# Gate phases of a retention + two-MoE kernel: products of neighbouring quads dealt out among each other, output products as filling, a shorter norm

## The chip, the cores and the metric

One core of a Trainium2 chip. The metric is the device time of one execution in microseconds, from the first to the last instruction and what lies around it; the median of three executions is given. The engines are named as in the profile: PE (TensorE), PEld (its weight loads), DVE (VectorE), ACT (ScalarE), POOL (GpSimd), SP (SyncE, which only issues transfers here).

## The reference

```
attn:  4 batches, 8 heads, 576 positions, head size 64:  ((q k^T / 8) * decay) v,  causal, no softmax
x   =  attn as 2304 tokens x 512
MoE 1: h = x @ w_in (512x2048);  g = h * cos(h);  x = g @ w_out (2048x512)
MoE 2: xn = x / sqrt(mean(x^2) + 1e-6) * rms_g
       out = (silu(xn @ w_gate) * (xn @ w_val)) @ w_out     (512x1536, 512x1536, 1536x512)
```

## The kernel before, in words

All products are fp32 made from three matmuls on high and low parts (`minus` makes a low part on DVE, after ACT has made the high one). The program runs attention, then MoE 1 over five token tiles in the order `ORDER_A` = 0, 1, 2, 4, 3 (four of 512 tokens, tile 4 of 256), then MoE 2 over three groups of 768 tokens (0, 1, 2). The weights of MoE 2 are prepared on the chip and stored to DRAM; later groups load them.

MoE 2 multiplies in Strassen's manner with seven products per 2x2 block. A *gate phase* has twelve *quads* (`quad`, even ones for the gate, odd ones for the value), each with seven products numbered 0 to 6 (`product`). A product is 2 x 3 matmuls of 128x128 weights on 384 columns. A quad owns two PSUM banks, alpha and beta: products 0, 2, 4 and 5 go to alpha, one on top of the other, and 1, 3 and 6 to beta. Between them the partial sum in alpha has to be copied out (`sums_of`: ACT's copies s1 after product 0, s2 after 2, s4 after 4), and `result` adds a sum and beta on DVE; for an even quad ACT takes the Silu of it, for an odd one DVE multiplies it with that Silu. So product 2 waits for s1's copy, product 3 for the add of result (0,0), product 4 for s2's copy, and a later quad's product for the add that last read its bank. Two quads later the banks come round again (`banks`). The order of PE is written out by hand: products 2, 3, 4 of quad q, then 0, 1 of quad q+1, then 5, 6 of quad q. The order of instructions on ACT, DVE and PE is that of the code (manual schedule).

In the *output phase* (`whole_out`) of a group seven `out_product`s of 54 matmuls with 256 columns each follow; the first begins inside the gate phase's end. `out_split` casts SV, the gate phase's result, into high and low parts, `block_out` adds up a block of the output into a tile `o` (two buffers) and stores it. `operand_steps(g+1)` makes the next group's seven token operands meanwhile.

In group 0 the weights of quads 2 to 11 are still made (`quad_steps`: ACT cast, DVE split, four POOL steps, two ACT casts, two DVE splits, two stores, and the fetch of another quad's input z; the first two steps of quad q+2 run after quad q's product 6). Ahead of that, in the last tile of MoE 1, the six output items (`out_steps`) and quads 0 and 1 are made in the same way. `ahead` puts their halves and the first group's operand steps into the list `ready`, which `other_steps` pulls in the order A, D, A, D, D (A an ACT step, D one of DVE) once for each of the sixteen steps of the tile. All output items go through the same staging tile `slots[0]`.

`norm(t)` makes the RMS norm of a tile in steps: squares (ACT), their sum (DVE), the mean over partitions (two matmuls with ones), an integer first guess of the inverse root, three Newton iterations of three DVE steps, and four scalings of x. It runs as `background` that `idle` takes up one step at a time: tiles 0, 1 and 2 in MoE 1, tiles 4 and 3 in group 1.

Of the kernel before, what the change touches and what calls it, by code (L numbers as in the profile page):

```python
# [22 lines left out]
F32 = mybir.dt.float32  # L23
# [7 lines left out]
P = 128  # L31
# [49 lines left out]
def body(ctx: ExitStack, tc, qkv, qkr, vr, w1, w2, rg, gq, gk, mask, out):  # L81
# [43 lines left out]
    spare = const.tile([P, 1], F32, name="spare")  # L125
    xall = const.tile([P, KC, NT], F32, name="xall")
# [94 lines left out]
    nc.vector.memset(quarter, 0.25)  # L221
    nc.gpsimd.memset(ones_r.bitcast(F32), 1.0)
# [94 lines left out]
    nc.sync.dma_start(rg_sb, rg)  # L317

# [4 lines left out]
    def norm(t):  # L323
# [21 lines left out]
        def mean():  # L345
            st["mean"] = acc_tile(0) if "S" in late else ps_tile()
            late["held"] = True
# [3 lines left out]

        def guess():
            late["held"] = False
            m, y = tmp(), tmp()
            nc.vector.tensor_scalar(m[:, :n], st["mean"][:, :n], 1.0 / DM, EPS, op0=ALU.mult, op1=ALU.add)
            nc.vector.tensor_scalar(y[:, :n].bitcast(I32), m[:, :n].bitcast(I32), -0.5, 1597463007.0,
                                    op0=ALU.mult, op1=ALU.add)
            st["m"], st["y"], st["u"] = m[:, :n], y[:, :n], tmp()[:, :n]

        def newton(step):  # L360
            m, y, u = st["m"], st["y"], st["u"]
            if step == 0:
                nc.vector.tensor_tensor(u, y, y, op=ALU.mult)
            elif step == 1:
                nc.vector.scalar_tensor_tensor(u, u, -0.5, m, op0=ALU.mult, op1=ALU.mult)
            else:
                nc.vector.scalar_tensor_tensor(y, u, 1.5, y, op0=ALU.add, op1=ALU.mult)
# [25 lines left out]
    def pull(engine):  # L393

        for steps in (background, ready) if late.get("held") else (ready, background):
# [114 lines left out]
    def operand_weights(q, plain, sums, keep_plain, keep):  # L510
# [17 lines left out]
        def low1():  # L528
            z = values_of.pop(q)
            for n in range(2):  # L530
                minus(nc.vector, sums[:, 1, 2 * n:2 * n + 2], sums[:, 0, 2 * n:2 * n + 2], z[:, 3 * n:3 * n + 2])
            keep()

        return [("A", high0), ("D", low0), ("A", high1), ("D", low1)]
# [84 lines left out]
    def ahead(i, n):  # L619
# [20 lines left out]
    def out_t(t, f):  # L640
# [9 lines left out]
        if f == NF1 - 1:  # L650
# [7 lines left out]
            if t not in ORDER_A[-2:]:  # L658
# [362 lines left out]
```

## Time and profile before

| | |
|---|---|
| median of three executions | 928.43 us (926.58 to 929.02) |
| the profiled execution | 930.18 us; its span, first to last instruction, 928.4 us |
| PE busy | 892.3 us, 96% of the span |
| DVE, ACT, POOL busy | 674.4, 474.6, 94.1 us |
| granted PE clock, mean | 0.993 of full speed |
| DMA | 189 MB, 204 GB/s over the span |

The stages of the span: attention and MoE 1 up to 494.1 us, gate phases from 494.1, 647.1 and 786.2, output phases from 606.1, 745.2 and 884.0. A row of a timeline has the start and the length in us, the engine, the line, the instruction with what it writes and reads, the count of merged instructions, and in brackets how long the engine stood before it and what ended that. Matmuls are pipelined and their ends are modelled: pace is read from start to start.

### The profile page before, as it was taken

What the parts mean: (1) busy time and instruction counts of PE and PEld (TensorE: products, weight loads), DVE (VectorE), ACT (ScalarE), POOL (GpSimd) and SP (SyncE); (2) the same over time, 40 slices, a digit from 0 to 9 for tenths busy, and PEclk for the clock granted to TensorE, in tenths of its full rate; (3) what the DMA queues carried; (4) which work ended last, traced back from release to release, by engine and by line L of the source; (5) the groups of instructions that cost most, each with busy time, mean ns of one, the idle gap of its engine ahead of it and who ended that gap; (6) DMA issues with size and microseconds to landing.
All of it is one profiled execution on the core that took longest, in us unless ns stands there. A gap on an engine that the chain in (4) does not pass through costs nothing.

```text
span 928.4 us, 14258 instructions
## 1 busy us (share of the span) xinstructions
PE 892.3 (96%) x5482; PEld 808.3 (87%) x5482; DVE 674.4 (73%) x1013; ACT 474.6 (51%) x813; POOL 94.1 (10%) x99
## 2 busy tenths in 40 slices
PE   7899999999999999999997999899999999999998
PEld 6788888888887888988886899899999999899998
DVE  3999989678788886678887576688467688343484
ACT  4666575566555664466554555444333344333341
POOL 2330100000000000002245333100000000000000
PEclk9999999999999999999999999999999999999999
DMA  8956261145434543104479788888666588666593
GB/s 335 413 213 247 102 250 47 34 140 163 140 101 125 147 141 89 46 7 133 144 229 322 265 295 291 320 289 274 242 238 241 213 290 281 235 238 243 211 291 118
DMA packets 59027, 188.98 MB, mean 204 GB/s; under 512 B 5328, under 2 KB 23376, under 8 KB 50384
## 3 DMA queue, kind: packets, MB, share of 16 engines
q1 hardware_dynamic: 58960, 188.08, 58.9%
q8 instruction: 43, 0.70, 0.3%
q14 instruction: 24, 0.20, 0.1%
HBM read 140.87 MB, written 47.19 MB: 203 GB/s over the span
## 4 chain that ended last, share of the span: by engine, by line
PE 60%; DVE 21%; ACT 7%; DMA 6%; issue 4%; SPq 1%; POOL 1%; ACTq 0%; DVEq 0%
PE acc L836 11%; PE h L771 11%; PE acc L771 11%; PE acc L192 5%; PE acc L193 5%; PE acc L194 5%; DVE w L129 3%; DVE r L429 2%; DVE t L147 2%; PE h L836 2%; DVE glo L129 2%; PE h L193 2%; PE h L194 2%; PE h L192 2%; DVE r L423 2%
## 5 line engine op out<-in xcount | busy, mean ns | idle before, releaser
L771 PE MATMUL h<-w 128*128 128x384 f32 x720 | 139.7, 344 | 9.7 <-DVE SV L780 5.4
L771 PE MATMUL acc<-w 128*128 128x384 f32 x720 | 137.1, 337 | 10.4 <-ACT s L756 10.3
L771 PEld LDWEIGHTS h<-w 128*128 128x128 f32 x720 | 128.8, 193 | 12.7 <-DVE SV L780 6.6
L771 PEld LDWEIGHTS acc<-w 128*128 128x128 f32 x720 | 126.0, 189 | 13.9 <-ACT s L756 13.6
L192 PE MATMUL acc<-ghi,w 128*128 128x512 f32 (+1 forms) x320 | 117.4, 373 | 2.7 <-ACT xall L652 1.7
L193 PE MATMUL acc<-glo,w 128*128 128x512 f32 (+1 forms) x320 | 117.8, 370 | 0.6 <-DVE glo L129 0.5
L194 PE MATMUL acc<-ghi,w 128*128 128x512 f32 (+1 forms) x320 | 117.4, 368 | 0.0
L836 PE MATMUL acc<-w 128*128 128x256 f32 x846 | 105.1, 285 | 0.0
L836 PEld LDWEIGHTS acc<-w 128*128 128x128 f32 x846 | 104.1, 194 | 0.2
L425 ACT ACTIVATE r<-r,half_pi 128x512 f32<-128x512 f32 (+1 forms) x80 | 54.5, 681 | 67.6 <-DVE r L423 67.3
L520 POOL TENSOR_TENSOR z<-z 128x256 f32<-128x256 f32 x72 | 64.5, 903 | 171.4 <-DMA z<-w 81.7
L129 DVE TENSOR_TENSOR glo<-r,ghi 128x512 fp32r<-128x512 f32 (+1 forms) x78 | 52.5, 673 | 35.4 <-ACT ghi L431 35.1
L431 ACT CAST ghi<-r 128x512 fp32r<-128x512 f32 (+1 forms) x80 | 46.2, 578 | 52.8 <-DVE r L429 50.9
L192 PEld LDWEIGHTS acc<-ghi,w 128*128 128x128 f32 x320 | 59.3, 188 | 14.5 <-ACT xall L652 2.6
L785 DVE TENSOR_TENSOR v<-s,acc 128x384 f32<-128x384 f32 x54 | 29.8, 551 | 57.7 <-ACT s L756 45.0
L193 PEld LDWEIGHTS acc<-glo,w 128*128 128x128 f32 x320 | 60.3, 188 | 11.0 <-DVE glo L129 1.2
L194 PEld LDWEIGHTS acc<-ghi,w 128*128 128x128 f32 x320 | 60.3, 188 | 10.1
L819 ACT CAST w<-SV 128x768 fp32r<-128x768 f32 x55 | 42.5, 832 | 41.3 <-DVE SV L787 23.1
L781 ACT ACTIVATE SV<-SV 128x384 f32<-128x384 f32 x54 | 28.4, 526 | 65.8 <-DVE SV L780 65.8
L780 DVE TENSOR_TENSOR SV<-s,h 128x384 f32<-128x384 f32 x54 | 29.7, 550 | 39.1 <-ACT s L756 31.2
L129 DVE TENSOR_TENSOR w<-SV,w 128x768 fp32r<-128x768 f32 x55 | 50.0, 951 | 9.9 <-ACT w L819 9.9
L756 ACT COPY s<-h 128x384 f32<-128x384 f32 x54 | 25.8, 477 | 56.1 <-PE h L771 56.1
(117 smaller groups left out, 1684.2 us busy)
## 6 DMA issues: line engine op xcount, KB each, us to landing
w<-so SPq DMA_DIRECT2D x42, 768.0 KB, 5.6
w<-s SPq DMA_DIRECT2D x24, 1024.0 KB, 4.9
raw<-w_dram SPq DMA_DIRECT2D x36, 512.0 KB, 4.2
w<-s SPq DMA_DIRECT2D x24, 768.0 KB, 6.0
raw<-w_dram SPq DMA_DIRECT2D x16, 1024.0 KB, 6.9
x<-qkv_dram SPq DMA_DIRECT2D x15, 1024.0 KB, 11.2
s<-w SPq DMA_DIRECT2D x12, 1024.0 KB, 6.3
w<-t SPq DMA_DIRECT2D x36, 256.0 KB, 2.4
```

The source lines that it names most:

```text
L129: eng.tensor_tensor(dst, src, hi.bitcast(F32), op=ALU.subtract)
L192: nc.tensor.matmul(dst, a[0], b[0], start=start, stop=False)
L193: nc.tensor.matmul(dst, a[0], b[1], start=False, stop=False)
L194: nc.tensor.matmul(dst, a[1], b[0], start=False, stop=stop)
L425: nc.scalar.activation(r, r, AF.Sin, bias=half_pi, scale=1.0)
L431: nc.scalar.copy(hi, r)
L520: nc.gpsimd.tensor_tensor(z[:, dst], z[:, a], z[:, b], op=op)
L771: nc.tensor.matmul(bank, a[:, wp], xp[:, c], start=start and kc == 0 and m == 0, stop=kc == 1 and m == 2, skip_group_check=True)
L780: nc.vector.tensor_tensor(dst, s, bank, op=ALU.add)
L785: nc.vector.tensor_tensor(t, s, bank, op=ALU.add)
L819: nc.scalar.copy(t[:, 0], src)
L836: nc.tensor.matmul(bank, s[:, a, i % 2, m * P:(m + 1) * P], wi[:, b], start=start and i == 0 and p == 0 and m % 2 == 0, stop=i == NPR - 1 ...
```

## The change

- `quad` becomes a class whose `product(k)` also does what follows the product on ACT and DVE. The loop deals two quads out among each other: 0, 1 of quad q, 5 of quad q-1, 2, 3 of q, 6 of q-1, 4 of q.
- A Silu goes to a list `waiting` and is issued right after the next sums copy (`flush`). s2 gets two buffers.
- In groups 1 and 2, where quad 0 has no quad before it, parts of the last output product of the group before stand in the places of 5 and 6; the last block's adds and store follow there. At the end of a gate phase the first 36 of the first output product's 54 matmuls, which stood in one piece ahead of products 5 and 6 of the last quad, stand in two pieces of 18 around product 5. The `o` tiles come from a pool of three.
- The output items are drawn more evenly, the second split of a quad's weights is cut into two steps, and the steps of `quad_steps` are spread over the seven places of a quad.
- The norm of the third tile of the order moves from the last tile of MoE 1 into group 0's gate phase (tiles 3 and 4 stay in group 1, in that order). Its iteration has seven DVE steps instead of nine; the mean's scaling and epsilon go to ACT; a factor 0.375 goes into `rg_sb` once.

```diff
-        steps += [("A", high), ("D", low), None, None, ("P", mean), None, None, ("D", guess)]
-        if t in ORDER_A[-2:]:
+        steps += [("A", high), ("D", low), None, None, ("P", mean), None, None, ("A", square_mean), ("D", guess)]
+        if t in ORDER_A[2:]:
...
-        steps += [("D", lambda s=s: newton(s)) for _ in range(3) for s in range(3)]
+        steps += [("D", lambda s=s: refine(s)) for s in range(7)]
...
-        for _ in range((n > 0) + (n in (8, 10, 12))):
+        for _ in range((n > 0) + (n % 3 == 0 < n)):
             ready.extend(next(halves, []))
-        if 1 <= n < 8:
+        if n in (1, 2, 4, 5, 7, 8, 10):
...
+    def flush():
+        while waiting:
+            waiting.pop(0)()
+
+    def sums_of(name, bank, width=GROUP):
+        t = sp.tile([P, width], F32, tag=name, name=name)
         nc.scalar.copy(t[:, :HALF], bank)
+        flush()
...
+        def product(self, k):
...
+            if k == 0:
+                self.s[1] = sums_of("s1", self.alpha)
+            elif k == 1:
+                self.result(0, 0, self.s[1], self.beta)
+            elif k == 2:
+                self.s[2] = sums_of(*(("s2", self.alpha) if self.q % 2 else ("s3", self.alpha, HALF)))
+            elif k == 4:
+                self.s[4] = sums_of("s4", self.alpha)
+                self.result(1, 1, self.s[4], self.beta)
+            elif k == 5:
+                self.result(0, 1, None, self.alpha)
+                flush()
+            elif k == 6:
+                self.result(1, 0, self.s[2], self.beta)
+                fetch(self.n + 3)
...
-        out_product(g, 6, delta, True)
-        block_out(g, 1, 0, s2, delta)
-        run(s[16:17])
...
+        out_product(g, 6, delta, True, range(NPR) if last else range(2))
...
+        def second():
+            out_product(g, 6, delta, True, range(4, NPR))
+            block_out(g, 1, 0, s2, delta)
+            late["last"] = s[16:]
+
+        late["fill"] = [lambda: out_product(g, 6, delta, True, range(2, 4)), second]
...
+            if q < NQUAD - 2 and k == 4:
+                items.append(quad_steps(q + 2))
+                run(items[-1][:1])
+            if 0 < q < NQUAD - 1:
+                run({0: items[-1][1:2], 3: items[-1][2:3], 6: items[-1][3:4]}.get(k, []))
+                if k == 4:
+                    run(items[-2 if q < NQUAD - 2 else -1][4:5])
...
+            now = Quad(g, q)
+            for k in (0, 1, 5, 2, 3, 6, 4):
+                if k < 5:
+                    now.product(k)
+                elif before:
+                    before.product(k)
+                elif fill:
+                    fill.pop(0)()
+                hook(g, q, k)
...
+                late["op"] = pool("op", 3)
+        late["alpha"] = [acc_tile(0), acc_tile(1)]
+        out_product(g, 0, late["alpha"], True, range(2))
+        hook(g, NQUAD, "first")
+        before.product(5)
+        out_product(g, 0, late["alpha"], True, range(2, 4))
+        before.product(6)
```

What this does to the order on the engines, at three places.

PE, from the end of group 0's output phase into group 1 (first before, then after). `h` and `acc` are the PSUM banks, 384 columns are gate products, 256 columns output matmuls.

```order
L836 MATMUL acc<-w 128x256 x144
L836 MATMUL acc<-w,b 128x256 x18
L836 MATMUL acc<-w 128x256 x18
L771 MATMUL h<-w 128x384 x30
L771 MATMUL acc<-w 128x384 x12
L771 MATMUL h<-w 128x384 x12
```

```order
L851 MATMUL acc<-w 128x256 x144
L806 MATMUL h<-w 128x384 x12
L851 MATMUL acc<-w,b 128x256 x18
L806 MATMUL h<-w 128x384 x12
L851 MATMUL acc<-w 128x256 x18
L806 MATMUL h<-w 128x384 x6
L806 MATMUL acc<-w 128x384 x12
```

The five products of quad 0 ran in one piece (30 matmuls); now 18 output matmuls stand after products 0, 1 and 18 more after 2, 3.

DVE at the same place: L862 and L877 are the adds of `block_out`, L780 and L788 the add of result (0,0) of quad 0.

```order
L862 TENSOR_TENSOR o<-s_5878,acc 128x256
L129 TENSOR_TENSOR w<-xall,w 128x768
L600 TENSOR_TENSOR xall<-xall 128x2x384
L129 TENSOR_TENSOR w<-xall,w 128x768 x2
L862 TENSOR_TENSOR o<-s_5746,acc 128x512
L862 TENSOR_TENSOR o<-s_5746,acc 128x256
L780 TENSOR_TENSOR SV<-s_5970,h 128x384
```

```order
L877 TENSOR_TENSOR o<-s_5878,acc 128x256
L130 TENSOR_TENSOR w<-xall,w 128x768
L610 TENSOR_TENSOR xall<-xall 128x2x384
L130 TENSOR_TENSOR w<-xall,w 128x768 x2
L788 TENSOR_TENSOR SV<-s_5926,h 128x384
L338 TENSOR_TENSOR nt<-nt 128x512
L877 TENSOR_TENSOR o<-s_5746,acc 128x512
L877 TENSOR_TENSOR o<-s_5746,acc 128x256
```

The add of quad 0 now stands ahead of the last block's adds.

ACT in the middle of group 0, from an even quad's s2 to the odd quad's s4. `s` are the sums copies, `SV<-` the Silus, `w<-z` the casts of `quad_steps`.

```order
L756 COPY s_5073<-h 128x384
L756 COPY s_5087<-h 128x384
L781 ACTIVATE SV<-SV 128x384
L526 CAST w<-z 128x512 x2
L756 COPY s_5106<-acc 128x384
L781 ACTIVATE SV<-h 128x384
L781 ACTIVATE SV<-SV 128x384
L514 CAST w<-z 128x768
L756 COPY s_5145<-acc 128x384
L756 COPY s_5159<-acc 128x384
```

```order
L772 COPY s_5052<-h 128x384
L535 CAST w<-z 128x512 x2
L772 COPY s_5079<-h 128x384
L523 CAST w<-z 128x768
L772 COPY s_5095<-acc 128x384
L790 ACTIVATE SV<-SV 128x384
L790 ACTIVATE SV<-h 128x384
L772 COPY s_5127<-acc 128x384
L535 CAST w<-z 128x512 x2
L772 COPY s_5152<-acc 128x384
L790 ACTIVATE SV<-SV 128x384
L523 CAST w<-z 128x768
```

The Silu that waits for product 6's add stood two places ahead of the odd quad's s2; it now stands behind that quad's s4.

## Rows read from the trace of the kernel before

**Rows 1.** The page: busy us, share of the span, instructions of each engine.

```profile
PE 892.3 (96%) x5482; PEld 808.3 (87%) x5482; DVE 674.4 (73%) x1013; ACT 474.6 (51%) x813; POOL 94.1 (10%) x99
```

**Rows 2.** The chain that ended last: start us, us, what.

```profile
496.19 4.49 DMA z<-w
...
695.03 2.08 PE acc L771 x12
```

**Rows 3.** Stages: us, busy us (instructions) of PE, PEld, DVE, ACT, POOL, granted clock, DMA.

```profile
410.00:494.10 84.10, 83.59 (x374) 68.71 (x372) 69.79 (x98) 52.49 (x85) 26.23 (x26) 1.00 0.52 164
494.10:606.10 112.00, 98.94 (x542) 94.22 (x541) 73.32 (x107) 54.95 (x106) 38.22 (x47) 0.97 0.82 295
606.10:647.10 41.00, 41.00 (x343) 40.92 (x343) 37.91 (x40) 19.87 (x29) 0.00 (x0) 1.00 0.88 290
647.10:745.20 98.10, 94.80 (x547) 93.80 (x546) 56.87 (x104) 36.33 (x75) 0.00 (x0) 0.98 0.65 234
786.20:884.00 97.80, 94.01 (x543) 93.36 (x542) 38.27 (x66) 32.26 (x65) 0.00 (x0) 0.98 0.65 234
```

**Rows 4.** The same view for the quads' matmuls alone (PE, PEld).

```profile
647.10:656.00 8.90, 7.12 (x31) 6.83 (x32) 0.81 0.84 305
656.00:736.00 80.00, 79.62 (x457) 78.74 (x455) 1.00 0.64 233
```

**Rows 5.** Timeline of PE, start of group 0.

```profile
496.19 0.62 PE L771 MATMUL h<-w 128*128 128x384 f32 x2 [1.77 <-ACT w L514]
...
501.06 4.97 PE L771 MATMUL h<-w 128*128 128x384 f32 x18 [1.87 <-ACT s L756]
...
516.45 2.25 PE L771 MATMUL h<-w 128*128 128x384 f32 x12
```

**Rows 6.** Groups of ACT, 480 to 505 us: busy us, mean ns, idle before.

```profile
L526 ACT CAST w<-z 128x512 fp32r<-128x512 f32 x6 | 3.6, 619 | 8.4 <-DMA so<-w 5.0 <-POOL z L520 3.4
```

**Rows 7.** Timeline of ACT, a pair of quads and the end of group 0.

```profile
529.92 0.81 ACT L514 CAST w<-z 128x768 fp32r<-128x768 f32 x1
530.65 0.47 ACT L756 COPY s<-acc 128x384 f32<-128x384 f32 x1
...
593.86 0.83 ACT L819 CAST w<-SV 128x768 fp32r<-128x768 f32 x1 [1.71 <-DVE SV L787]
```

**Rows 8.** Timeline of PE, gaps after that.

```profile
531.17 1.32 PE L771 MATMUL acc<-w 128*128 128x384 f32 x6 [1.02 <-ACT s L756]
...
597.12 1.59 PE L771 MATMUL acc<-w 128*128 128x384 f32 x6 [2.50 <-ACT s L756]
...
652.17 3.88 PE L771 MATMUL h<-w 128*128 128x384 f32 x12 [1.75 <-DVE SV L780]
...
737.60 1.33 PE L771 MATMUL acc<-w 128*128 128x384 f32 x6 [1.54 <-ACT s L756]
...
791.75 3.59 PE L771 MATMUL h<-w 128*128 128x384 f32 x12 [2.26 <-DVE SV L780]
```

**Rows 9.** Timeline of DVE, start of group 1.

```profile
650.64 1.02 DVE L862 TENSOR_TENSOR o<-s,acc 128x512 f32<-128x512 f32 x2 [4.04 <-DMA out_dram<-o]
651.57 0.55 DVE L780 TENSOR_TENSOR SV<-s,h 128x384 f32<-128x384 f32 x1
```

**Rows 10.** A pair of quads in group 0, columns as in rows 3.

```profile
531.00:546.70 15.70, 14.86 (x84) 14.50 (x84) 10.57 (x17) 8.68 (x18) 6.01 (x8) 1.00 0.86 306
```

**Rows 11.** A norm step on DVE, 470 to 512 us: ns, min/median/max.

```profile
L363 DVE TENSOR_TENSOR nt<-nt x2: 680/952/1225, 471.3 to 491.5; 128x512 f32<-128x512 f32 x2
```

**Rows 12.** Timeline of POOL, one quad's four steps.

```profile
531.88 3.27 POOL L520 TENSOR_TENSOR z<-z 128x256 f32<-128x256 f32 x4 [5.40 <-DVE w L129]
```

**Rows 13.** Transfers issued from 470 to 610 us: KB each, us to landing.

```profile
so<-w SPq DMA_DIRECT2D x15, 256.0 KB, 4.7
```

**Rows 14.** Timeline of ACT, the second cast of quad 0's weights.

```profile
499.50 1.14 ACT L526 CAST w<-z 128x512 fp32r<-128x512 f32 x2 [3.36 <-POOL z L520]
```

**Rows 15.** Loads of quad weights in group 1, issue to landing.

```profile
DMA to landing us min/median/max: 4.6/5.3/6.8
```

More of the change, by code (lines that the diff above doesn't have):

```diff
@@ L393, in pull @@
     def pull(engine):
-        for steps in (background, ready) if late.get("held") else (ready, background):
+        for steps in (ready, background):
             if steps and steps[0] and steps[0][0] == engine:
@@ L526, in high1, with low1 @@
                 nc.scalar.copy(sums[:, 0, 2 * n:2 * n + 2], z[:, 3 * n:3 * n + 2])
[L528 to L534, printed above, removed]
+        def low1(n):
+            z = values_of[q]
+            minus(nc.vector, sums[:, 1, 2 * n:2 * n + 2], sums[:, 0, 2 * n:2 * n + 2], z[:, 3 * n:3 * n + 2])
+            if n:
+                del values_of[q]
+                keep()
+        return [("A", high0), ("D", low0), ("A", high1), ("D", lambda: low1(0)), ("D", lambda: low1(1))]
     where = lambda q: 3 * (q // 2) + q % 2
@@ L733, in body @@
         ready.pop(0)[1]()
+    assert not background and next(halves, None) is None
     staging.close()
@@ L752, in run, with __init__, result @@
             step()
-    def sums_of(name, bank):
-        t = sp.tile([P, GROUP], F32, tag=name, name=name)
+    def flush():
[3 more added lines that the diff above has]
+        t = sp.tile([P, width], F32, tag=name, name=name)
         nc.scalar.copy(t[:, :HALF], bank)
+        flush()
         return t[:, :HALF]
-    def quad(g, q, hook):
-        val, j = q % 2, q // 2
-        n = g * ITEMS + q
-        alpha, beta = (t[:, :HALF] for t in banks())
-        plain, sums = side(n)
-        def product(bank, w, k, start):
-            home, xhi, xlo = ops[g, k]
-            for kc in range(2):
-                a, c = w[..., kc * P:(kc + 1) * P], kc
-                for m, (wp, xp) in enumerate(((0, xhi), (0, xlo), (1, xhi))):
-                    nc.tensor.matmul(bank, a[:, wp], xp[:, c], start=start and kc == 0 and m == 0,
-                                     stop=kc == 1 and m == 2, skip_group_check=True)
-            if q == NQUAD - 1:
-                places.append(home)
-        def result(u, h, s, bank):
-            dst = SV[:, j, u, h]
-            if not val:
+    class Quad:
+        def __init__(self, g, q):
+            self.g, self.q, self.n = g, q, g * ITEMS + q
+            self.plain, self.sums = side(self.n)
+            self.alpha, self.beta = (t[:, :HALF] for t in banks())
+            self.s = {}
+        def result(self, u, h, s, bank):
+            dst = SV[:, self.q // 2, u, h]
+            if self.q % 2 == 0:
                 if s is not None:
                     nc.vector.tensor_tensor(dst, s, bank, op=ALU.add)
-                nc.scalar.activation(dst, bank if s is None else dst, AF.Silu)
+                    bank = dst
+                waiting.append(lambda: nc.scalar.activation(dst, bank, AF.Silu))
             else:
@@ L859, in block_out @@
     def block_out(g, dm, half, a, pair):
-        o = gp.tile([P, GROUP], F32, tag="o", name="o")
+        o = late["op"].tile([P, GROUP], F32, tag="o", name="o")
         for c, bank in zip(PARTS, pair):
@@ new lines, in body @@
+    items = []
+    for g in range(NGROUP):
+        assert not background
+        for t in (ORDER_A[2:3], ORDER_A[:2:-1], [])[g]:
+            background.extend(norm(t))
+        fill = late.pop("fill", [])
+        before = None
+        for q in range(NQUAD):
+            now = Quad(g, q)
[7 more added lines that the diff above has]
+                hook(g, q, k)
+            before = now
+            if g == 0 and q == NQUAD - 2:
```

133 lines of the change are left out of this document (57 added, 76 removed).

## The prediction, made before the changed kernel ran

> **What bounds the kernel now.** I read the page's busy shares first, then the stages in one windows view, then for each stage that loses time the timelines of the engines that TensorE (PE) waits for. PE is busy 96% of 928.4 us, DVE 73%, ACT 51% [rows 1], so only stretches where PE is not at its own pace can be won. One product of a quad is 6 matmuls; 12 of them run back to back in 2.08 us [rows 2], so a product takes 1.04, and an output matmul 41.0 / 343 = 0.12 [rows 3]. Each of the three gate phases has 84 products and the first 36 output matmuls: 87.4 + 4.3 = 91.7 us. They take 112.0, 98.1 and 97.8 [rows 3]; the second also holds the matmuls of two norm means (some 0.7). The loss is 20.3 + 5.7 + 6.1 = 32 us. The output phases (41.0 busy of 41.0) and the middle of group 1's gate phase (79.62 of 80.0) lose nothing [rows 3, 4]. The change is judged by what it takes from those 32 us.
>
> **Where the 32 us are.** *Start of group 0* (494.1 to 516.45): 12 products, 12.5 us of work, in 22.35: 9.9 lost. PE waits 1.77 for quad 0's weights and 1.87 for a sums copy, and then 18 matmuls take 4.97 where 12 take 2.25 at pace [rows 5]: after such gaps the granted clock falls from the upper of its two levels (2.4 GHz) to the lower (1.2); the mean over the stretch of the like gap in group 1 is 0.81 [rows 4]. Ahead of those weights stand ACT's waits for stores to land, because all six output items go through one staging tile: 5.0 us [rows 6]. *Rest of group 0*: 72 products and the 36 matmuls, 79.2 us, take 89.65: 10.4 lost. The repeating part: after an even quad ACT runs, in order, the Silu of product 6's result, quad q+2's first weight cast (0.81) and only then the copy of product 2's partial sum, which PE's product 4 awaits: 1.02 us of gap in the pair of quads shown [rows 7, 8], and about as much in every pair. At the end, ACT waits 1.71 for DVE before a cast that stands ahead of the same copy; PE stands 2.50 [rows 7, 8], and the slow matmuls behind the gap cost more. *Groups 1 and 2*: at the start DVE stands 4.04 us for an output store that still reads one of two o tiles, with the add that frees product 1's bank queued behind it. PE waits 1.75 and 2.26, then needs 3.88 and 3.59 for 12 matmuls: 3.4 and 3.6 lost. At the end of group 1 the same queue on ACT costs 1.54 again [rows 8, 9], and I take group 2 for like it.
>
> **The change, part by part.**
>
> *Start of groups 1 and 2.* The o pool has three tiles, so the last block writes the tile whose store went out with the group's first block, some 20 us before, and DVE's wait goes. Two thirds of the last output product move to where a preceding quad's products 5 and 6 would stand; the same 54 matmuls run. What is late next: product 3 needs the add of result (0,0). From the end of the fourth output product DVE has two blocks' o adds, three weight splits and a difference to do, about 6.7 us with the copy before them (the two adds of a block take 1.02 [rows 9]; a split or difference of 768 columns some 0.95, an estimate, a little under twice the 0.55 of a 384-column add there), and PE passes 2.2 + 2.1 + 2.2 + 1.0 = 7.5 before product 3. Then quad 1's product 0 takes over the bank that the last block's adds (1.02) read, with one product between: at best even. I leave 0.5 us for both. Gain 2.9 and 3.1; bounds 1.5 each (a wait of 2 us comes back) and the whole 3.4 and 3.6.
>
> *End of the gate phases.* Product 4 now follows product 2 after two others (3 of its own quad, 6 of the one before), 2.08 us, where 1.04 stood, and the casts of the output's first operand stand behind the copies. I leave 0.2 at each end. Gain 1.3 in groups 1 and 2 each, bounds 0.5 and 1.7. Their middles, without loss today, can only lose: each bank now has 2.08 us from one product's end to the next one's start on it. A copy and an add of 384 columns, 0.47 and 0.55 [rows 7, 9], with some 0.3 to start, fit in; I book nothing.
>
> *Rest of group 0.* The Silu is put off until behind the next copy, so the repeating wait goes. What is late next is DVE. In the pair of quads from 531.0 to 546.7 it is busy 10.57 of 15.7 us [rows 10]; at PE's pace a pair has 14.57. The norm of the third tile moves here: 16 DVE steps, two or three a quad in quads 5 to 9. The same steps took 0.68 alone and 1.22 beside POOL [rows 11]. Five a pair make 10.57 + 3.4 = 14.0 to 10.57 + 6.1 = 16.7: 0 to 2.1 over PE's pace. POOL works 3.27 us of a quad's 7.3 [rows 12], so some half of the steps meet it: 1.1 a pair, 2.7 for two and a half pairs, and about 1 for order in the other quads. With 0.3 for the end, 4.0 of the 10.4 stay: gain 6.4, bounds 1 (every step beside POOL and ahead of an add that frees a bank) and 9.5.
> On that the Trainium skill (SBUF — State Buffer, Who interferes with whom) has a rule that speaks against the move: a DVE instruction with two SBUF inputs and a GpSimd instruction that reads SBUF shut each other out for a whole instruction. The trace agrees in kind, 0.68 against 1.22. By the rule each of the 16 could be held for one POOL step, 3.27 / 4 = 0.82, which makes 13 us of DVE; by the rows' difference it is 16 × 0.54 = 8.6 at most.
>
> *Start of group 0.* The output items are drawn at steps 3, 6, 9 and 12 of the last tile rather than 8, 10 and 12, so item 4's sums cast stands two steps before item 5's, some 10.8 us (48 matmuls at 84.1 / 374 = 0.225 [rows 3]), where one step stood. A store lands 4.7 us after issue [rows 13], and its four issues take some 2: 6.7, inside two steps and outside one. The 5.0 us of waits go. In their place: PE runs products 0 and 1 from about 494. Product 2 needs the copy of product 0, which now stands behind quad 1's first cast. That waits for its input, which is fetched when item 5's weights are done and lands 4.5 us later [rows 2]; it was asked for at 496.2 and is now some 3.8 earlier (most of the 5.0; behind item 5's first cast POOL's work takes the place of the stores), so it lands at 497. With 0.83 and 0.48 for cast and copy product 2 can start at 498.4; before, it began at 501.06 [rows 5]. Product 4's copy now stands behind quad 1's second cast, which waits for POOL as quad 0's does (3.36 [rows 14]), so it ends near 503.5. From there eight products without a wait bring the twelfth to 511.8 instead of 516.45. Gain 4.7, bounds 0 (the waits only move) and 7.
>
> *The norm itself.* Nine steps of Newton become seven, and ACT takes the mean's scaling: DVE loses three steps of 0.68 a tile, ACT gains one. Up to 494.1 PE is busy 83.59 of 84.1 [rows 3], so there is next to nothing to win, and slack on both engines covers the added ACT step: 0 to 0.5. Without that cover it would cost 0.6 for each of two tiles.
>
> **Sum.** 2.9 + 3.1 + 1.3 + 1.3 + 6.4 + 4.7 = 19.7. The profiled execution took 930.18 us, so 910.5; it lay 1.75 above the median of the runs, 928.43, so **908.7 us** for the median.
>
> **Rivals.**
> *A, DVE becomes the bound of group 0.* If most norm steps meet POOL and stand ahead of adds that free banks, quads 5 to 9 run at 8.3 us, and the start of the group gains little (ACT has new squares there). Against it: DVE has 5.1 us spare in a pair today. Gain 2.9 + 3.1 + 2.6 + 1 + 2 = 11.6: 916.8.
> *B, one wait takes the place of another at the starts.* The banks of the last output product are read in quad 0's middle; if its adds come late there, quad 1 stands as quad 0 did. For it: by the count above DVE's queue there is full to within a microsecond. The starts then win 1.5 each, and with A's losses the gain is near 8: 920.
> *C, slower: weights arrive late.* A quad's weight buffer is freed by product 6, and eight products (8.3 us) rather than ten (10.4) now pass before quad q+3 needs it. Loads land 4.6 to 6.8 us after issue [rows 15]. It decides from 8.3 us on; at 9.4 each of 20 quads in groups 1 and 2 would stand 1.1, which takes back more than the whole gain: 931. Against it: the longest seen leaves 1.5 us.
> *D, nothing:* the order changes but each wait stays, 928. Against it: the wait for the o tile has a named buffer, and a third tile removes it.
>
> **How the numbers follow.** Forecast 0.62, A 0.20, B 0.08, C 0.06, D 0.04. The forecast's own range, with the bounds of its terms taken half way, is 904 to 913. To leave out no more than 2 in 10 the range takes in A and some of the low side: **902 to 918**. A measurement of this kernel can tell about 0.3%, 2.8 us, from no change. Faster: forecast, A and B, 0.90; same: D, 0.04; slower: C, 0.06.
>
> **What would show it.** Gate phases of about 101, 94 and 93 us; no DVE wait on an output store; no ACT wait on the staging tile's stores; no gap after an even quad. The start of group 0 should keep two gaps of 2 to 3 us. Wrong if DVE is busy over 95% in the middle of group 0, if PE in groups 1 and 2 waits for a load, or if new waits on DVE appear at quad 1.

## The result, and the profile after

The changed kernel takes 904.31 us (median of 4 runs, 903.15 to 907.02) against 927.55 (926.58 to 929.02) for the kernel before beside it: a ratio of 0.9752, 95% interval 0.9725 to 0.978, 23.2 us less. The forecast was 908.7, its whole range 902 to 918. The profiled execution took 904.74 us.

The page's line of the engines, which answers to [rows 1]:

```profile
PE 883.7 (98%) x5482; PEld 804.6 (89%) x5482; DVE 669.0 (74%) x999; ACT 478.3 (53%) x819; POOL 96.3 (11%) x99
```

The stages, columns as in [rows 3]: from the end of MoE 1 to group 0's twelfth product, the rest of that gate phase, output phase and next gate phase of groups 0/1 and of groups 1/2. First after the change, then the same stretches before it.

```profile
492.95:509.82 16.87, 13.37 (x73) 12.40 (x73) 9.91 (x13) 11.70 (x23) 9.01 (x12) 1.00 1.00 381
509.82:591.81 81.99, 81.31 (x473) 79.34 (x472) 69.31 (x102) 45.93 (x87) 30.05 (x34) 1.00 0.85 309
591.81:725.56 133.75, 133.64 (x888) 133.16 (x888) 92.10 (x138) 56.89 (x106) 0.00 (x0) 1.00 0.78 262
725.56:858.69 133.13, 133.02 (x884) 132.62 (x884) 76.38 (x106) 51.83 (x94) 0.00 (x0) 1.00 0.79 261
```

```profile
494.10:516.45 22.35, 15.94 (x75) 14.01 (x74) 16.26 (x20) 9.49 (x18) 10.04 (x10) 0.92 0.87 312
516.45:606.10 89.65, 83.00 (x469) 80.21 (x469) 57.06 (x87) 45.47 (x88) 28.18 (x38) 0.98 0.81 291
606.10:745.16 139.06, 135.76 (x887) 134.68 (x887) 94.78 (x144) 56.20 (x104) 0.00 (x0) 0.99 0.71 250
745.16:883.97 138.81, 135.02 (x884) 134.29 (x883) 76.18 (x106) 52.16 (x94) 0.00 (x0) 0.99 0.72 250
```

After the change PE is busy all but 0.1 us in the last two stages: nothing is left of the gaps at the starts and ends of groups 1 and 2 [rows 8]. Where PE still waits is the start of group 0. Its timeline there, and below the dots the only two gaps that the view shows later in group 0:

```profile
492.79 2.27 PE L806 MATMUL h<-w 128*128 128x384 f32 x12
496.36 1.33 PE L806 MATMUL h<-w 128*128 128x384 f32 x6 [1.30 <-ACT s L772]
498.46 1.34 PE L806 MATMUL h<-w 128*128 128x384 f32 x6 [0.78 <-DVE SV L788]
501.23 1.31 PE L806 MATMUL h<-w 128*128 128x384 f32 x6 [1.43 <-ACT s L772]
...
541.02 1.31 PE L806 MATMUL h<-w 128*128 128x384 f32 x6 [0.25 <-DVE SV L788]
544.69 1.32 PE L806 MATMUL h<-w 128*128 128x384 f32 x6 [0.28 <-DVE SV L788]
```

Before, quad 0 began with a wait for its weights (1.77) and the copy's gap was 1.87 with 18 slow matmuls behind it [rows 5]; now there are three gaps of at most 1.43, and the granted clock stays at the upper level (1.00 for 0.92). ACT's casts of the weights:

```profile
488.38 1.14 ACT L535 CAST w<-z 128x512 fp32r<-128x512 f32 x2 [0.71 <-POOL z L529]
494.06 1.14 ACT L535 CAST w<-z 128x512 fp32r<-128x512 f32 x2 [3.06 <-POOL z L529]
499.66 1.14 ACT L535 CAST w<-z 128x512 fp32r<-128x512 f32 x2 [2.34 <-POOL z L529]
```

They wait for POOL alone; the 5.0 us for stores [rows 6] are gone from this stretch. Waits of 0.84 and 1.44 for stores are left earlier in the last tile of MoE 1, at 457.0 and 479.4 us. Two pairs of quads in which the moved norm runs, same columns as the stages:

```profile
539.60:555.50 15.90, 15.38 (x85) 14.44 (x84) 15.47 (x23) 8.38 (x16) 7.08 (x9) 1.00 0.80 292
555.50:570.30 14.80, 14.80 (x85) 14.49 (x85) 14.66 (x22) 8.35 (x16) 6.88 (x9) 1.00 0.89 319
```

DVE is busy 97 and 99% there (10.57 of 15.7 before [rows 10]). That is the sign I had named for a wrong prediction, and yet PE lost little. Its gaps on DVE's adds in this stretch are the 0.25 and 0.28 above, and read from start to start each of them costs 0.5. The two pairs take 15.9 and 14.8 us where PE's pace makes 14.57.

### The profile page after: what moved, and what is told of

Read it like the earlier page. It is cut to its first block, busy times and chain, and to the rows that moved or that the text cites. A ratio compares the mean times of both kernels' runs of the same rounds, so it can differ in the third digit from the quotient of the medians.

```text
span 902.9 us, 14216 instructions
## 1 busy us (share of the span) xinstructions
PE 883.7 (98%) x5482; PEld 804.6 (89%) x5482; DVE 669.0 (74%) x999; ACT 478.3 (53%) x819; POOL 96.3 (11%) x99
## 4 chain that ended last, share of the span: by engine, by line
PE 78%; DVE 14%; ACT 3%; issue 2%; DMA 1%; POOL 1%; SPq 0%; ACTq 0%; DVEq 0%; POOLq 0%
PE h L806 13%; PE acc L806 13%; PE acc L851 13%; PE acc L193 8%; PE acc L194 8%; PE acc L195 8%; PE h L193 3%; PE h L194 3%; PE h L195 3%; DVE w L130 3%; PE h L851 2%; DVE t L148 2%; DMA x<-qkv_dram 1%; DVE t L149 1%; PE g L287 1%
## 5 line engine op out<-in xcount | busy, mean ns | idle before, releaser
L806 PE MATMUL acc<-w 128*128 128x384 f32 x720 | 140.1, 335 | 0.4
L806 PEld LDWEIGHTS h<-w 128*128 128x128 f32 x720 | 125.7, 188 | 5.9 <-ACT s L772 3.4
L851 PEld LDWEIGHTS acc<-w 128*128 128x128 f32 x846 | 103.1, 191 | 0.3 <-DVE w L130 0.2
L193 PEld LDWEIGHTS acc<-ghi,w 128*128 128x128 f32 x320 | 60.3, 188 | 12.5 <-ACT xall L662 2.0
L193 PE MATMUL h<-xhi,w 128*128 128x512 f32 (+1 forms) x144 | 52.7, 366 | 0.0
L193 PE MATMUL acc<-xhi,w 128*128 128x512 f32 (+1 forms) x144 | 52.7, 366 | 0.0
## 6 DMA issues: line engine op xcount, KB each, us to landing
x<-qkv_dram SPq DMA_DIRECT2D x15, 1024.0 KB, 11.4
```

The costliest lines, as they stand in the source:

```text
L193: nc.tensor.matmul(dst, a[0], b[0], start=start, stop=False)
L806: nc.tensor.matmul(bank, w[:, wp, kc * P:(kc + 1) * P], x[:, kc], start=k in (0, 1, 3) and kc == 0 and m == 0, stop=kc == 1 and m == 2, sk ...
L851: nc.tensor.matmul(bank, s[:, a, i % 2, m * P:(m + 1) * P], wi[:, b], start=start and i == 0 and p == 0 and m % 2 == 0, stop=i == NPR - 1 ...
```

## The experiments

The change has five parts that could each hold the gain: the third output tile, the filling, the put-off Silu, the drawing with the moved norm, and the order of the products with the new places of the operand steps. My theory was the prediction's: third tile for the starts of groups 1 and 2, Silu for the middle of group 0, drawing for its start, order for the ends. The rivals were that one part does most of it, and that a part works only beside another. Eight runs add parts to the kernel before or take them from the changed one; four more followed from what these showed.

The stages of one profiled execution each, read from PE's timeline: from the end of MoE 1's last matmul to the end of the 72nd gate matmul ("start"), from there to the last gate matmul ("rest"), and from one group's last gate matmul to the next's. Work without any wait is 12.5, 79.2, 133.4 and 132.7 us, by the prediction's paces and with 0.7 for the norm means in group 1.

| kernel | median | before beside it | start, rest of group 0 | sum | group 1 | group 2 |
|---|---|---|---|---|---|---|
| before | | 927.55 | 22.2, 89.7 | 111.9 | 139.1 | 138.8 |
| + third tile | 923.55 | 926.69 | 21.9, 89.7 | 111.6 | 135.6 | 134.7 |
| + put-off Silu | 915.28 | 926.69 | 20.2, 82.9 | 103.1 | 133.7 | 133.3 |
| + put-off Silu, groups 1 and 2 only | 923.42 | 927.58 | 21.7, 88.2 | 109.9 | 136.5 | 134.0 |
| + third tile, put-off Silu | 913.00 | 926.69 | 20.6, 84.5 | 105.1 | 133.7 | 133.2 |
| + drawing | 928.53 | 926.69 | 22.0, 89.8 | 111.8 | 137.9 | 139.1 |
| + drawing, moved norm | 926.86 | 927.58 | 14.4, 97.2 | 111.6 | 137.8 | 138.3 |
| + all four, old order | 908.42 | 927.58 | 12.6, 89.9 | 102.5 | 133.8 | 133.3 |
| changed | 904.31 | 927.55 | 16.9, 82.0 | 98.9 | 133.7 | 133.1 |
| changed, two o tiles | 906.05 | 928.26 | 18.4, 82.5 | 100.9 | 133.8 | 133.3 |
| changed, no filling | 903.94 | 928.26 | 18.4, 82.5 | 100.9 | 133.7 | 133.3 |
| changed, Silu at once | 911.47 | 928.26 | 19.7, 85.3 | 105.0 | 133.9 | 133.3 |
| changed, old drawing | 908.82 | 928.26 | 20.9, 82.5 | 103.4 | 133.7 | 133.1 |
| changed, quad 1's steps later | 902.75 | 927.58 | 15.6, 82.4 | 98.0 | 133.7 | 133.1 |

Kernels that are alike up to a point differ there by up to 2 us in group 0 (the third tile cannot matter before its output phase, yet 16.9 stands beside 18.4 and 103.1 beside 105.1), and the end of MoE 1 fell between 491.6 and 496.7 us in all these executions. A difference of 2 us in group 0 is therefore not read; in groups 1 and 2 like stages agree to 0.2. One execution also need not be like the median of its runs: the kernel before took 930.18 us in the profiled one, and the one with the Silu put off 913.03, the fastest of its four. So the stages say where a gain lies, and the runs how large it is. The ratios below are those on record with their intervals; they are near the quotients of the medians, but not the same.

**The third tile alone.**

```diff
-        o = gp.tile([P, GROUP], F32, tag="o", name="o")
+        o = late["op"].tile([P, GROUP], F32, tag="o", name="o")
...
+                late["op"] = pool("op", 3)
```

> The kernel before with only the output tiles changed: they come from a pool of three, the rest as it was. Theory: the wait of DVE for an output store (4.04 and 4.54 us) is the whole of the loss at the starts of groups 1 and 2, and a third tile alone removes it: DVE then has the last block's adds done some 2 us before product 3 of quad 0 needs its add, so 6 to 7 us are gained (3.4 and 3.6 less at most 0.5 each), about 921. Rival 1: DVE's queue there is so full that PE waits again without the filling; gain 3 us or less, 924.5 or more. Rival 2: the store itself holds something else, no gain, 927.5.

923.55 us, ratio 0.9951 (0.9934 to 0.9969): 4.5 us faster by the ratio, 3.1 by the medians, and 3.5 + 4.1 in the two stages. The time lies between the theory's and rival 1's, so the rows decide. No gap of PE is left at either start, and the add that stood 4.04 us [rows 9] now waits 0.37 for PE's last output matmul. So the mechanism stands, and rivals 1 and 2 fall.

```profile
648.97 1.02 DVE L862 TENSOR_TENSOR o<-s,acc 128x512 f32<-128x512 f32 x2 [0.37 <-PE acc L836]
```

**The put-off Silu alone.**

```diff
+    def flush():
+        while waiting:
+            waiting.pop(0)()
...
         nc.scalar.copy(t[:, :HALF], bank)
+        flush()
...
-                nc.scalar.activation(dst, bank if s is None else dst, AF.Silu)
+                waiting.append(lambda: nc.scalar.activation(dst, bank if s is None else dst, AF.Silu))
...
         result(0, 1, None, alpha)
+        flush()
```

> The kernel before with only the Silu put off until behind the next sums copy (and behind product 5's result); order of products, pools and drawing as before. Theory: the repeating gap of about 1.02 us in every pair of quads of group 0 comes from the Silu that waits for product 6's add ahead of the copy, so five pairs give 4 to 5 us, about 923; the ends of groups 1 and 2 keep their 1.5 us, the starts theirs. Rival: the weight cast (0.81 us) that stays ahead of the same copy keeps most of the gap, and only the new order of products takes it away: gain below 2 us, 926 or more.

915.28 us, ratio 0.9864 (0.9828 to 0.9899): 12.6 us by the ratio, 11.4 by the medians, over twice what I expected. Besides 6.8 us in the rest of group 0 it takes both ends of groups 1 and 2, and both starts. The end of group 1 shows why; ACT there in the kernel before:

```profile
736.66 0.52 ACT L781 ACTIVATE SV<-SV 128x384 f32<-128x384 f32 x1 [1.10 <-DVE SV L780]
737.09 0.46 ACT L756 COPY s<-acc 128x384 f32<-128x384 f32 x1
```

and the same copy with the Silu put off:

```profile
725.22 0.48 ACT L761 COPY s<-acc 128x384 f32<-128x384 f32 x1 [1.17 <-DVE SV L786]
725.59 0.53 ACT L787 ACTIVATE SV<-SV 128x384 f32<-128x384 f32 x1
```

The copy (s2 of the last quad) that PE waits for stood behind a Silu which waited 1.10 us for an add. Now the copy goes first. It still waits for the same add, which reads the one s2 tile that the copy writes, but saves the Silu's time. The add is done sooner, too: ACT goes on from it 1.8 us after PE has left product 6 (at 723.43) instead of 2.85 (at 733.81), because a cast for the output, whose split stands ahead of the add on DVE, no longer stands behind another Silu. Only the end of group 0 keeps its gap (2.17 us).

**Both together.** The two edits above.

> The kernel before with both the pool of three output tiles and the put-off Silu. If the two parts act in different stages they add up: the sum of the gains of the two alone, by the theories 10 to 12 us, about 916. If the new order of the products is needed for either, less than 7 us, 920 or more.

913.00 us, ratio 0.9842 (0.9811 to 0.9873): 14.6 us less, not the sum of 4.5 and 12.6 that the ratios gave singly, though the intervals are wide. The stages say it plainly: groups 1 and 2 are at 133.7 and 133.2 with the Silu alone, so the third tile finds nothing left there.

**The Silu put off in groups 1 and 2 only.** With two o tiles; `if g` decides whether the Silu is put off.

```diff
+                act = lambda: nc.scalar.activation(dst, bank if s is None else dst, AF.Silu)
+                waiting.append(act) if g else act()
```

> The kernel before with the Silu put off in groups 1 and 2 only, group 0 as it was, two output tiles. With the Silu put off everywhere no wait of PE was left at the starts of groups 1 and 2, though the third tile was missing. Theory: this is local (the Silu of quad 0's first result no longer stands on ACT ahead of product 2's copy): both starts are free of gaps here, and with the ends of the gate phases some 5 to 7 us are gained, 920 to 922. Rival: the output store lands earlier because of what went before in the preceding gate phase: group 1's start keeps DVE's wait of about 4 us and PE's gap of about 1.8, group 2's has none, and the gain is 3.5 to 5 us, 922 to 923.5.

923.42 us, ratio 0.9938 (0.9904 to 0.9972). The rival holds, but for one small gap: at group 1's start DVE stands 4.78 us for the store and PE 2.50; at group 2's start DVE does not stand for a store, and PE stands 0.52, which the rival had at nothing. The rows of DVE, then of PE:

```profile
650.05 1.02 DVE L870 TENSOR_TENSOR o<-s,acc 128x512 f32<-128x512 f32 x2 [4.78 <-DMA out_dram<-o]
```

```profile
651.59 2.35 PE L777 MATMUL h<-w 128*128 128x384 f32 x12 [2.50 <-DVE SV L786]
...
786.17 2.35 PE L777 MATMUL h<-w 128*128 128x384 f32 x12 [0.52 <-DVE SV L786]
```

So what the put-off Silu wins at the starts comes from a store that lands earlier, not from the order on ACT at the spot. With the Silu put off everywhere DVE still stands 2.0 us for it at group 1's start, which PE does not feel. The four stores of the two blocks ahead, issued at like distances from the end of the output phase, landed 8.9 us after issue (median) in group 0 here and 6.6 in group 1; 8.1 and 8.7 in the kernel before, 6.1 and 6.0 with the Silu put off everywhere. What holds them in the first case is not settled by any run; with both edits together they took 8.3 in group 1 and nothing waited, thanks to the third tile.

**The changed kernel with two o tiles.** `pool("op", 2)`.

> The changed kernel with two output tiles instead of three; filling, order and all else as changed. Theory: the wait of DVE for an output store comes back with the pool of two, and PE waits behind it: 3 us or so at the start of each of groups 1 and 2, about 910. Rival: the filling (36 matmuls of the last output product among quad 0's products) puts the last block's adds so late that the store has landed by then, and the pool of three was not needed: less than 1 us, 904 to 905.

906.05 us, ratio 0.9757 (0.9737 to 0.9776). The time lies between the theory's 910 and the rival's 904 to 905, but the theory falls: DVE waits for no store and there is no gap at either start; the stages of groups 1 and 2 differ from the changed kernel's by 0.2 at most. Whether the filling does that, as the rival had it, or the put-off Silu, this run cannot tell.

**The changed kernel without the filling.** The last output product in one piece ahead of quad 0, with its block's adds.

```diff
-        out_product(g, 6, delta, True, range(NPR) if last else range(2))
-        if last:
-            block_out(g, 1, 0, s2, delta)
-            return
+        out_product(g, 6, delta, True, range(NPR))
+        block_out(g, 1, 0, s2, delta)
+        late["last"] = s[16:]
+        return
```

> The changed kernel without the filling at the starts of groups 1 and 2: the last output product runs in one piece ahead of quad 0 and its block's adds stand ahead of quad 0's, with the pool of three kept. Theory: the third tile is what matters, DVE's queue passes in time or up to 0.5 us late at each start: 0 to 1 us, 904 to 905.5. Rival: with products 0 and 1 and then 2 of quad 0 in a row and no product between them, PE waits for copies and adds at each start, 1 to 3 us each: 906.5 to 910.

903.94 us, ratio 0.9743 (0.9714 to 0.9771), no gap at either start. The third tile and the put-off Silu each cover the starts alone, as the runs above show; the filling may be a third cover, but was not tried without them. With several covers, taking away one shows nothing.

**The changed kernel with the Silu at once.**

```diff
-                waiting.append(lambda: nc.scalar.activation(dst, bank, AF.Silu))
+                nc.scalar.activation(dst, bank, AF.Silu)
```

> The changed kernel with each Silu issued at once, where it stands in the code, instead of behind the next sums copy. Theory: the Silu ahead of a copy is what stopped PE after each even quad; with two products between any two of one bank it still waits for product 6's add, so in group 0 about 0.5 to 1 us comes back in each of five or six pairs: 3 to 6 us, 907 to 910. Rival: two other products (2.08 us instead of 1.04) cover Silu and copy together, and the order alone is enough: less than 1 us, 904 to 905.5.

911.47 us, ratio 0.9816 (0.9797 to 0.9834): 7.2 us over the changed kernel, more than the 3 to 6 of the theory. Gaps behind even quads are back, up to 1.04 us, and the rest of group 0 takes 85.3 us instead of 82.0, but the ends of groups 1 and 2 stay free. So the order of the products, with the casts' new places, covers the ends by itself, as the put-off Silu does; in group 0 it does not replace it.

**The drawing alone, and taken away.** The first puts the two new lines into the kernel before, the second puts the old ones into the changed kernel.

```diff
-        for _ in range((n > 0) + (n in (8, 10, 12))):
+        for _ in range((n > 0) + (n % 3 == 0 < n)):
...
-        if 1 <= n < 8:
+        if n in (1, 2, 4, 5, 7, 8, 10):
```

> The kernel before with only the drawing of the output items and operand steps changed (items at steps 3, 6, 9 and 12, operand steps at 1, 2, 4, 5, 7, 8, 10); the norm of the third tile stays in the last tile of MoE 1, and the quads' order is as before. Theory: the start of group 0 loses 9.9 us because ACT stands 5.0 us for the stores of the staging tile; drawn evenly these waits go, and about 5 us are gained, all of it before the twelfth product of group 0, about 922.5. Rival: the waits go but the steps that follow (the norm's own in the last tile, quad 1's casts behind quad 0's) keep the start, and the gain is 0 to 2 us, 926 or more.

> The changed kernel with the drawing of the output items and operand steps as before (items at steps 8, 10 and 12, operand steps at 1 to 7). Theory: the staging tile's store waits on ACT come back and delay the weights of quad 0: 4 to 6 us at the start of group 0, 908 to 910. Rival: with the norm of the third tile gone from the last tile of MoE 1, ACT and DVE have room and the drawing matters little: less than 1.5 us, up to 906.

Alone: 928.53 us, ratio 1.0 (0.9977 to 1.0024), nothing. Taken away: 908.82, ratio 0.979 (0.9769 to 0.981), 4.5 us over the changed kernel, with PE standing 4.51 us for quad 0's weights. The runs answer each other. Alone, the waits of ACT's second casts for stores shrink from 5.0 to 1.1 us, but PE then stands 4.75 us for the add of product 1, and this is DVE ahead of that add:

```profile
498.78 1.22 DVE L365 SCALAR_TENSOR_TENSOR nt<-nt 128x512 f32<-128x512 f32 x1
500.03 0.69 DVE L367 SCALAR_TENSOR_TENSOR nt<-nt 128x512 f32<-128x512 f32 x1
500.76 2.74 DVE L370 SCALAR_TENSOR_TENSOR xall<-xall,rg_sb,nt 128x512 f32<-128x512 f32 x4
503.42 0.55 DVE L780 TENSOR_TENSOR SV<-s,h 128x384 f32<-128x384 f32 x1
```

The third tile's norm steps and scalings stand there, late.

Nor do the stores by themselves set the start. The kernel with the third tile alone has the program of the kernel before up to here. In the view of [rows 6] its second casts read:

```profile
L526 ACT CAST w<-z 128x512 fp32r<-128x512 f32 x8 | 4.8, 618 | 8.0 <-POOL z L520 6.7 <-DMA so<-w 1.3
```

ACT stood 8.0 us instead of 8.4, with only 1.3 of it put down to stores instead of 5.0, and the start took 21.9 us instead of 22.2. A wait is put down to what ended it last, and here POOL and the store ended close together. With the drawing taken away from the changed kernel, too, ACT stands 2.6 us for stores in all, little more than the 2.3 with it. What the drawing changes is how early the weights of quads 0 and 1 are made.

**Drawing and moved norm.** The lines above, and the norm of the third tile in group 0's gate phase.

```diff
-            if t not in ORDER_A[-2:]:
+            if t in ORDER_A[:2]:
                 background.extend(norm(t))
...
+        for t in (ORDER_A[2:3], ORDER_A[-2:], [])[g]:
+            background.extend(norm(t))
```

> The kernel before with the new drawing and with the norm of the third tile moved from the last tile of MoE 1 into group 0's gate phase (old norm iteration, old order of products, Silu at once, two output tiles). Theory: drawing alone gained nothing because the norm's steps and scalings, late on DVE, took the place of the store waits (4.75 us of wait for product 1's add); with both, the twelfth product of group 0 comes some 17 to 18.5 us after the end of MoE 1 instead of 22, 3.5 to 5 us gained there, of which the norm's steps in the quads give back up to 2: 923 to 926. Rival: the start needs the new order or the put-off Silu as well: twelfth product after 21 us or more, 926.5 or more.

926.86 us, ratio 0.9982 (0.9955 to 1.0009): within its uncertainty of nothing. By its stages half of it is as the theory had it: the start takes 14.4 us, better than in the changed kernel, without the order or the put-off Silu. But the rest takes 97.2, 7.5 more than before, where the theory gave up to 2. ACT in a quad of that stretch, then the PE rows:

```profile
531.54 0.52 ACT L781 ACTIVATE SV<-SV 128x384 f32<-128x384 f32 x1 [2.90 <-DVE SV L780]
531.97 0.82 ACT L514 CAST w<-z 128x768 fp32r<-128x768 f32 x1
533.15 0.48 ACT L756 COPY s<-h 128x384 f32<-128x384 f32 x1 [0.36 <-DVE v L785]
```

```profile
524.19 1.33 PE L771 MATMUL acc<-w 128*128 128x384 f32 x6 [2.00 <-ACT s L756]
...
544.81 1.31 PE L771 MATMUL acc<-w 128*128 128x384 f32 x6 [2.05 <-ACT s L756]
```

With the norm's steps ahead of the adds on DVE, the Silu waits longer (2.90 us), and the gap after an even quad grows from the 1.02 of [rows 8] to 2.0.

**All four in the old order.** Third tile, put-off Silu, drawing and moved norm; without the new order, the filling, the new places of a quad's operand steps, the cut in its second split and the short norm.

> The kernel before with third output tile, put-off Silu, new drawing and moved norm together, but with the old order of the products, no filling, the old norm iteration and the operand steps of a quad in the old places. Theory: the order of the products buys next to nothing where the Silu is put off and the drawing with the moved norm gives 4 us at the start of group 0: 907 to 910. Rival: two other products between any two of one bank are needed against the norm's steps in group 0 (DVE 97 to 99% busy there) and at the gate phases' ends: 911 or more, the gap to the changed kernel's 904.3 staying 6.5 us or more.

908.42 us, ratio 0.9765 (0.9735 to 0.9796): 4.1 us above the changed kernel, in the span that the theory gave, but not for its reason. Its start has no loss at all (12.6), its rest 10.7, among it 2.17 at the end of the phase, as with the Silu alone, and five gaps of 0.5 to 1.0 between 521 and 541 us, where the norm runs (3.8 in all; slower matmuls behind them, with a mean granted clock of 0.98 over the rest, add to it). In the changed kernel the gaps there come to 0.53 and the end has none. So the order, with the new places of the operand steps, is worth 7.9 us in the rest; the two weren't tried apart, nor was the short norm. The difference of the runs is only 4.1, because the changed kernel loses 4.3 at the start (16.9, and 18.4 in the two kernels that are alike there) where this one loses nothing. ACT's casts here, of quad 0 (the second), quad 1 (the first) and quad 1 (the second):

```profile
489.47 1.13 ACT L526 CAST w<-z 128x512 fp32r<-128x512 f32 x2
490.50 0.83 ACT L514 CAST w<-z 128x768 fp32r<-128x768 f32 x1
494.54 1.14 ACT L526 CAST w<-z 128x512 fp32r<-128x512 f32 x2 [3.21 <-POOL z L520]
```

MoE 1 ends at 494.2 in this kernel, so only quad 1's second cast comes later. In the changed kernel MoE 1 ends at 492.95, and quad 0's second cast (494.06) and both of quad 1 come behind that. The drawing is the same in both. What differs in making these items is the second split cut into two steps: each item then has three DVE steps, all that `other_steps` pulls in one step of the tile, and the operand steps stand in the same list. That this cut is what makes the items late is argued from the code; no run tried the changed kernel without it.

**The second half of quad 1's operand steps behind quad 0's products,** in the changed kernel: in the start of group 0 two of the three gaps were copies behind weight casts.

```diff
-                yield steps[2:]
+                if make is quad_steps and j == 1:
+                    late["second"] = steps[2:]
+                else:
+                    yield steps[2:]
...
+            if q == 0 and k in (2, 6, 4):
+                run({2: late["second"][:1], 6: late["second"][1:2], 4: late["second"][2:]}[k])
```

> The changed kernel with the second half of quad 1's operand steps (two ACT casts that wait for POOL, two DVE splits) moved behind quad 0's products: the casts after product 2's copy, the first split in the free place after product 3, the second after product 4. Theory: the three gaps of PE at the start of group 0 (1.30, 0.78 and 1.43 us) are waits for copies and an add that stand behind these casts and splits; 1.5 to 2.5 us of the 4.4 lost there come back: 902 to 903. Rival: the weights of quad 0, which wait for POOL, and then quad 1's sums, now made later, set the start: no change within 0.5 us, 904 to 905.

902.75 us (902.68 to 902.85), ratio 0.9703 (0.967 to 0.9737), faster than both kernels by the median; its interval overlaps the changed kernel's. The time is as the theory had it, 902 to 903. The gap ahead of product 4 is gone and the other two remain:

```profile
495.32 1.31 PE L809 MATMUL h<-w 128*128 128x384 f32 x6 [1.30 <-ACT s L775]
497.43 2.35 PE L809 MATMUL h<-w 128*128 128x384 f32 x12 [0.79 <-DVE SV L791]
```

The first copy still stands behind quad 0's cast and quad 1's first one. The start takes 15.6 us instead of 16.9, a difference that is within the scatter named above; the missing gap is the surer sign. Its four runs lie within 0.2 us, with a granted clock of 0.998 to 1.0 over the whole, while the changed kernel's spread over 3.9, the slowest with 0.994 and the fastest with 1.0.

## Why the prediction was right, and where its reasons were not

The total held: 19.7 us were forecast; the profiled executions give 25.4, of which 1.5 lie ahead of the stages, and the medians beside each other 23.2. The time is at the low edge of the forecast's own range, 904 to 913. By its own terms:

- **Starts of groups 1 and 2** (2.9 + 3.1). The size was right, and the third tile does it alone. The 0.5 us that I left at each for a full DVE queue did not come. What I did not see is that the put-off Silu suffices too, so the term cannot be put down to the third tile within this change.
- **Ends of the gate phases** (1.3 + 1.3). Here the cause was too narrow. I gave them to the order and the casts' new place; the copy stood behind a Silu waiting for its add, and the put-off Silu alone removes it, as the order does without it. Starts and ends together were forecast at 4.2 and 4.4 and came to 5.3 and 5.7, all but 0.4 of what there was to lose.
- **Rest of group 0** (6.4). It gave 7.7. The put-off Silu alone gives most of that, as I said (6.8; 5.2 beside the third tile), but it does not carry it by itself: without it the changed kernel still keeps 4.3. The norm's cost was mis-sized. I booked 2.7 us for it as if a full DVE costs PE by itself. Already by its own rows that was too much: with half of the five steps of a pair beside POOL they make 10.57 + 2.5 × 0.68 + 2.5 × 1.22 = 15.3, which is 0.75 over PE's pace and not 1.1. In the old order the rest is 5.4 to 7.5 longer with the norm (84.5 to 89.9, 89.7 to 97.2); in the new one DVE at 97 to 99% costs about 1 us. I put that down to the two products that now stand between any two of one bank, so that the adds have more time; the order was not tried apart from the new places.
- **Start of group 0** (4.7). It gave 5.3 in this execution and 3.8 in the two that are alike there. The waits that I took over from the changed order on ACT came: the copies behind quad 1's two casts are the gaps of 1.30 and 1.43. The step that failed is the reason for the gain: I gave the whole to the drawing and to ACT's waits for stores. The drawing alone gives nothing, because the norm's late steps then hold DVE ahead of the first add, and most of the 5.0 us would have been spent waiting for POOL without the stores, as the kernel with the third tile alone shows. The moved norm, which I booked only as a cost in the quads, is what lets the drawing pay. Together they are worth 7.8 to 9.6 in the old order (14.4 and 12.6 for 22.2). That the changed kernel gets about half of it, and so the forecast's size, is luck.
- **The norm itself** (0). The shorter iteration was not tried alone. The end of MoE 1 came 1.5 us earlier than before, within the scatter of like kernels, so it is not claimed.

The gate phases, forecast at 101, 94 and 93 us, took 98.9, 92.7 and 92.1 (stages less 41.0 for an output phase). Rival A came true in its condition (DVE full in the middle) and not in its price. Rival B's wait did not come. For rival C, no wait of PE for a load shows in group 1 or 2. On the rule of the Trainium skill (SBUF — State Buffer, Who interferes with whom) the changed kernel's trace agrees in kind again: the squaring step of the norm's iteration on DVE took 694 and 1222 ns in group 0, so 0.53 more, less than the whole POOL step of 0.82 that the prediction worked out by it.

## What to carry to other kernels

On an in-order engine, put what waits for another engine behind what TensorE waits for: moving one Silu behind one copy was worth 11 to 13 of the 23 us, without any new order of products. Before booking a gain to one part, look at what stands next in that queue: here the drawing paid at the start only once the norm was out of its way. In the old order the norm's new place then took all of it back, while with the Silu put off and the third tile the two together brought 913.00 down to 908.42. And where several covers lie over one wait, taking one away measures nothing; add each alone to the kernel before.

## What the runs showed of the hardware that was not expected

The same four output stores, issued at like distances from the end of the output phase, landed 8.1 to 8.9 us after issue in some groups and kernels and 6.0 to 6.6 in others (medians); in this kernel a wait on a store's landing is not a constant. And here a gap a little longer cost more than itself. From 487 to 512 us, columns as in the stages, the changed kernel, whose gap ahead of product 4 is 1.43 us:

```profile
487.00:512.00 25.00, 21.50 (x113) 19.51 (x112) 15.24 (x20) 16.98 (x33) 13.24 (x16) 1.00 0.86 315
```

and the one with two o tiles, the same program in this stretch, with 1.96 us there and 1.51 ahead of it:

```profile
487.00:512.00 25.00, 21.49 (x105) 19.70 (x104) 13.87 (x20) 16.16 (x31) 13.48 (x15) 0.93 0.82 308
```

The gaps sum to 3.47 us in the second and to 3.51 in the first, and yet its start of group 0 took 18.4 us instead of 16.9: the granted clock fell from the upper level (2.4 GHz) to the lower (1.2) for a while, 0.93 in the mean. Behind the gap of 1.96 us two products take 3.80 us where they take 2.24 in the changed kernel. The kernel without the filling, with gaps of 1.60 and 1.98, did the same (0.93, 18.4). It is what separates 16.9 from 18.4 in the table: the idle time is the same.
